# Two heads of wo loaded with 8 as the source's outermost dimension, and three short tables with 4

## The chip, the cores and the metric

The kernel runs on one core of a Trainium2 chip. The metric is the device time of one execution in microseconds (us); before the change three runs gave 1271.48, 1272.16 and 1272.31, so the median is 1272.16.

The engines are named as the profile names them: PE does matrix multiplications (PEld is its weight load), DVE is the vector engine, ACT the scalar engine, POOL is GpSimd, and SP only issues transfers and waits. Every transfer between the memory outside (HBM) and the on-chip memory (SBUF) is done by the core's 16 DMA engines. An instruction on SP or ACT describes a whole transfer; it is cut into packets that the DMA engines then carry out. In this text a "DMA engine" is one of those 16, and "engine" alone is a compute engine or SP.

## The reference

Two results are mixed by a gate. The first is one decode step of grouped-query attention: one token of width 448, 16 query heads, 8 key/value heads with 65,536 cached rows of 256 numbers each. The second is a layer norm of the token with a small two-layer map of hidden width 1792.

```python
g = sigmoid((x * gate_w).sum(-1))
q = (x @ wq).reshape(16, 256)                      # per head
p = softmax(q[h] . k_cache[h // 2] / 16)           # over 65,536 rows
a = concat_h(p @ v_cache[h // 2]) @ wo             # wo is 4096 x 448
h = layernorm(x)
b = (gelu(h[:, None] * w1[0] + b1) @ w2 + b2)      # one number for each of 448
out = g * a + (1 - g) * b
```

All inputs and the output are bf16. The two caches are 268 MB each, together 537 of the 544 MB that the kernel reads.

## The kernel before

**Blocks.** The 65,536 rows of each of the 8 key/value heads are worked off in 4 blocks of 16,384, so there are 32 blocks, n = 0 to 31 (the loop at L529). A partition holds 128 rows that follow each other in the cache, so a block's K is two tiles of 128 partitions x 64 rows (`kn0` and `kn1`, 4 MB each, loaded by `load_k`, L113), and its V is one tile of 128 x 128 rows (`vt`, 8 MB, `load_v`, L120). Each partition's share is contiguous in memory.

**A block's work.** For each of 8 groups of rows DVE transposes a piece of K (L354) and PE multiplies it with the queries (L362). After the last group comes the softmax (L416 to L455: DVE, PE and ACT by turns), and then PE multiplies the probabilities with V (L384); DVE adds the product to `acc` (L459, L464).

**Order.** Nothing is scheduled: the helper `seq` (L60) chains every instruction to the one before it on its engine, so each engine works in the order of the text. An instruction that waits holds up all that stands behind it on its engine. On SP's queue the order is: wq in two loads (L142, L143), K of block 0 in three (L152, L153), then for each block n: V of block n, the first half of K of block n+1, the second half; and at n = 0 after these the output weights wo of the first 14 heads (L541, `load_wo`, L128). V of block n is loaded when PE is done with V of block n-1, and half of K when DVE has transposed what was in its tile.

**Semaphores of loads.** Eight semaphores tell of the landing of loads, given out in turn to the loads of SP and ACT together, in the order of the text. A load that gets a semaphore again first waits until the load eight places before it has landed. In the program's list of waits this reads, for the first loads on SP: the first load of K waits for xr (L141), the second for the large part of wq (L142), the third, which is the second half of K of block 0 (L153), for w1b (L147), V of block 0 for b1b (L148), the first half of K of block 1 for w2b (L149), the second for gw (L150).

**The short tables.** ACT issues six small loads at the start: the token xr (one row of 896 bytes), w1b, b1b and w2b (L147 to L149; each 128 partitions x 14 numbers, that is 128 rows of 28 bytes), the gate's weights gw (one row of 896 bytes) and b2b (one number). DVE converts w1b and b1b at L240 and L241. Behind these two in DVE's order stand the rest of the layer norm (L242 to L250), the copies of the queries (L281, L290, L295) and all transposes of K. ACT's GELU of 14 x (128 x 448) (L255) uses both tables; PE uses w2b at L321, in `mixer_tail`, which is called in the midst of block 0.

**wo and the end of a head.** `wo_sb` holds wo with two rows (c = 0, 1) of a head on each partition: partition p of head h holds rows 2p and 2p+1 of that head's 256, 1792 contiguous bytes. When the four blocks of a key/value head are done (n = 3, 7, ...), `denominators` and `head_end` (L497) run: `collect` (L478) turns `acc` by four small matmuls, taking even columns for c = 0 and odd for c = 1, so that the product's partition p matches wo's row pair p; then `project` (L488) multiplies with wo and DVE adds up (L504, L506). The last key/value head is finished otherwise, at the program's end (L583 to L610), with wo of the last two heads loaded one by one (L550).

Of the kernel before, what the change touches and what calls it, by code (L numbers as in the profile page):

```python
# [8 lines left out]
FP32 = mybir.dt.float32  # L9
# [5 lines left out]
HQ = 16  # L15
HKV = 8
DH = 256
REP = HQ // HKV
# [6 lines left out]
NQ = 4  # L25
NW = DH // 2 // 32
QW = 128 + 2 * NI


@with_exitstack  # L30
def kernel(
# [15 lines left out]
    nc = tc.nc  # L47
# [5 lines left out]
    NF = F // 128  # L53
# [6 lines left out]
    def seq(ins):  # L60
        e = ins.ins.engine
        if e in last:
            tc.add_manual_dep(
                ins.ins,
                last[e],
                mybir.DependencyInfo(
                    mybir.DependencyClass.NoSync, mybir.DependencyReason.DATA
                ),
                reason="program order",
            )  # L70
        last[e] = ins.ins.name
        return ins
# [3 lines left out]
    work = ctx.enter_context(tc.tile_pool(name="work", bufs=1))  # L76
# [9 lines left out]
    wo_sb = const.tile([128, HQ, 2, D], BF16)  # L86
# [13 lines left out]
    w1b = const.tile([128, NF], BF16)  # L100
    b1b = const.tile([128, NF], BF16)
    w2b = const.tile([128, NF], BF16)
# [6 lines left out]
    def rows(cache, n):  # L109
        g, b = divmod(n, NB)  # L110
        return cache[0, g, b * BLK:(b + 1) * BLK, :].rearrange("(p j) d -> p j d", j=VP)
# [16 lines left out]
    def load_wo(h0, h1):  # L128
        seq(nc.sync.dma_start(
            out=wo_sb[:, h0:h1],  # L130
            in_=A_wo[h0 * DH:h1 * DH, :].rearrange("(h p c) n -> p h c n", p=128, c=2),
        ))

    def load_v_last(n):
        for j0, j1 in LAST:
            seq(nc.sync.dma_start(
                out=k_tiles[j0 // KP][:, j0 % KP:(j1 - 1) % KP + 1, :],
                in_=rows(A_v_cache, n)[:, j0:j1, :],
            ))
# [4 lines left out]
        out=wq_t[:, :], in_=A_wq[DM:D, :].rearrange("r (h n) -> (r h) n", h=2)  # L144
    ))
    with nc.allow_non_contiguous_dma(reason="short rows"):
        seq(nc.scalar.dma_start(out=w1b[:], in_=B_w1[0].rearrange("(p b) -> p b", b=NF)))  # L147
        seq(nc.scalar.dma_start(out=b1b[:], in_=B_b1.rearrange("(p b) -> p b", b=NF)))  # L148
        seq(nc.scalar.dma_start(out=w2b[:], in_=B_w2.rearrange("(p b) o -> p (b o)", b=NF)))  # L149
        seq(nc.scalar.dma_start(out=gw[:], in_=gate_w.rearrange("(o n) -> o n", o=1)))  # L150
        seq(nc.scalar.dma_start(out=b2b[:], in_=B_b2.rearrange("(o n) -> o n", o=1)))
    load_k(0, 0, ((0, 32), (32, KP)))  # L152
# [10 lines left out]
        out=val[:], in_=rowsel[:, :, :, 0:NI], op=ALU.add, axis=AXIS.XY  # L163
    ))
    fst = const.tile([128, 2, REP], FP32)
    for e in range(2):
        seq(nc.vector.tensor_reduce(
            out=fst[:, e, :], in_=rowsel[:, :, :, e:e + 1], op=ALU.add, axis=AXIS.XY
# [3 lines left out]
        out=par[:], in_=ident_f[:].rearrange("p (a r) -> p r a", r=REP), op=ALU.add, axis=AXIS.X  # L172
# [3 lines left out]
        out=nval[:], in0=val[:], scalar1=-scale, scalar2=None, op0=ALU.mult  # L176
# [7 lines left out]
        out=same[:], in_=val[:].unsqueeze(1).to_broadcast([128, 64, REP])  # L184
    ))
    seq(nc.vector.memset(pv_ps[:], 0.0))
    seq(nc.vector.memset(pv_last[:], 0.0))
    qz_tiles = [const.tile([128, 2 * NW, QW], BF16, name=f"qz{i}") for i in range(2)]
    for i in range(2):
# [3 lines left out]
        out=sel[:],  # L193
        in_=ident[:].rearrange("p (w k) -> p w k", w=NW).unsqueeze(2).to_broadcast([128, NW, NQ, 32]),
# [7 lines left out]
        out=xrr[:], in_=xr[:, DM:D].unsqueeze(2).to_broadcast([1, D - DM, 2])  # L202
    ))
    x_col = hd_ps[:, 40:44]
    for k in range(3):
# [13 lines left out]
        out=xtm[:], in0=par[:], scalar1=x_col[:, 3:4], scalar2=None, op0=ALU.mult  # L219
# [17 lines left out]
        out=veps[:], in0=mv[:, 1:2], scalar1=1e-5, scalar2=None, op0=ALU.add  # L237
# [5 lines left out]
    for _ in range(2):  # L243
# [3 lines left out]
            out=ntmp[:], in0=ntmp[:], scalar1=-0.5, scalar2=1.5, op0=ALU.mult, op1=ALU.add  # L247
# [3 lines left out]
        out=h_bc[:], in0=xf[:], scalar1=mv[:, 0:1], scalar2=rstd[:, 0:1],  # L251
        op0=ALU.subtract, op1=ALU.mult,
    ))
    for b in range(NF):
        seq(nc.scalar.activation(  # L255
            out=gel[:, b, :], in_=h_bc[:], func=ACT.Gelu_apprx_tanh,
# [4 lines left out]
    for h in range(HQ):  # L261
        half, hh = divmod(h, HQ // 2)
        for c in range(2):
            col = c * HQ + h
            for k in range(3):
                seq(nc.tensor.matmul(
                    q_ps[:, col:col + 1],
                    lhsT=wq_m[:, k, h * DH:(h + 1) * DH].rearrange("p (d c) -> p c d", c=2)[:, c, :],
                    rhs=xm[:, k:k + 1],
                    start=(k == 0),  # L270
                    stop=False,
# [3 lines left out]
                lhsT=wq_t[:, hh * DH:(hh + 1) * DH].rearrange("p (d c) -> p c d", c=2)[:, c, :],  # L275
                rhs=xtm[:, half:half + 1],
                start=False,
                stop=True,
# [4 lines left out]
    for w in range(NW):  # L283
        seq(nc.tensor.matmul(
            qq_ps[:, w * 2 * HQ:(w + 1) * 2 * HQ],
            lhsT=sel[:, w, :, :].rearrange("p a k -> p (a k)"), rhs=qb[:],
            start=True, stop=True,
# [44 lines left out]


    acc = work.tile([128, 2, DH], FP32)
    lsum = work.tile([128, 1], FP32)
    mrun = work.tile([1, REP], FP32)
    mnew = work.tile([1, REP], FP32)
# [8 lines left out]
    esc = work.tile([128, 2, REP], FP32)  # L346
# [128 lines left out]

    o_ps = [hd_ps[:, 464:464 + REP], sm_ps[:, 464:464 + REP]]

    def collect(weights, start, stop):  # L478
        for c in range(2):
            for e in range(2):  # L480
                seq(nc.tensor.matmul(  # L481
                    o_ps[c],
                    lhsT=acc[:, e, :].rearrange("p (d c) -> p c d", c=2)[:, c, :],
                    rhs=weights[:, e, :],
                    start=(start and e == 0), stop=(stop and e == 1),
                ))

    def project(g):  # L488
        a_ps = hd_ps[0:1, 0:D]
        for r in range(REP):  # L490
            for c in range(2):
                seq(nc.tensor.matmul(  # L492
                    a_ps, lhsT=oT[:, c, r:r + 1], rhs=wo_sb[:, g * REP + r, c, :],
                    start=(r == 0 and c == 0), stop=(r == REP - 1 and c == 1),
                ))

    def head_end(g):  # L497
        collect(esc, True, True)
        for c in range(2):
            seq(nc.vector.tensor_copy(out=oT[:, c, :], in_=o_ps[c]))  # L500
        project(g)
        a_ps = hd_ps[0:1, 0:D]
        if g == 0:
            seq(nc.vector.tensor_copy(out=a_acc[:], in_=a_ps))  # L504
        else:
            seq(nc.vector.tensor_tensor(out=a_acc[:], in0=a_acc[:], in1=a_ps, op=ALU.add))  # L506
# [22 lines left out]
    for n in range(NBLK):  # L529
        if n == 0:  # L530
            score_block(n, {2: gate_sum, 5: mixer_tail})
        elif n < L:
            score_block(n, {1: gate_column} if n == 1 else {})
        else:
            score_block(n, {1: result_base, 2: lambda: pv(L - 1, 0), 3: lambda: pv_one(L - 1, 2)})
        if n < L - 1:
            load_v(n)
            load_k(n + 1, 0)
            load_k(n + 1, 1)
            if n == 0:  # L540
                load_wo(0, HQ - REP)  # L541
        elif n == L - 1:
            load_v(n, 0, 48)
            load_k(L, 0)
            load_k(L, 1)
            load_v(n, 48, VP)
        else:
            load_v_last(L)
            for h in range(HQ - REP, HQ):
                load_wo(h, h + 1)  # L550
        if n < L:
            softmax(n)
        else:
            def rest_base():
                for k in range(2):
                    seq(nc.tensor.matmul(
                        f_rows[k], lhsT=ident_f[0:1, 0:1], rhs=base[0:1, k * MC:(k + 1) * MC],
                        start=True, stop=False, tile_position=(0, 32 * k),
                    ))
                pv(L - 1, 2, range(4, NJ))  # L560

            softmax(n, [lambda: pv_one(L - 1, 3), lambda: pv(L - 1, 2, range(4)), rest_base])
            seq(nc.vector.tensor_scalar(
                out=lsv[:], in0=val[:], scalar1=lsum[:, 0:1], scalar2=None, op0=ALU.mult
            ))
            pv(L - 1, 3)
            accumulate(L - 1)
            seq(nc.tensor.matmul(
                sm_ps[:, 456:456 + REP], lhsT=ones_f[:, :], rhs=lsv[:, :], start=True, stop=True
            ))  # L570
            seq(nc.vector.reciprocal(out=rdv[:], in_=sm_ps[:, 456:456 + REP]))
            seq(nc.vector.tensor_scalar(
                out=rdv[:], in0=rdv[:], scalar1=gcol[:, 0:1], scalar2=None, op0=ALU.mult
            ))
        if n < L - 1:
            if n % NB == NB - 1:
                denominators()
            products(n)
            if n % NB == NB - 1:
                head_end(n // NB)  # L580
# [6 lines left out]
    for c in range(2):  # L587
        for e in range(2):
            seq(nc.tensor.matmul(
                o_last[:, c, :],  # L590
                lhsT=acc[:, e, :].rearrange("p (d c) -> p c d", c=2)[:, c, :],
                rhs=fst[:, e, :],
                start=False, stop=False, skip_group_check=True,
# [3 lines left out]
        out=oT[:], in0=o_last, in1=rdv[:].unsqueeze(1).to_broadcast([128, 2, REP]), op=ALU.mult  # L597
    ))
    for r in range(REP):
        for c in range(2):  # L600
            for k in range(2):
# [3 lines left out]
                    start=False, stop=(r == REP - 1 and c == 1),  # L605
# [35 lines left out]
```

## Time and profile before

| what | value |
|---|---|
| median of three runs | 1272.16 us (1271.48 to 1272.31) |
| span of the profiled execution | 1270.1 us; a whole time of its own is not listed, the median is 2.06 above the span |
| PE busy | 785.6 us, 62% of the span |
| DVE busy | 683.8 us, 54% |
| ACT busy | 43.1 us, 3% |
| read from HBM | 544.22 MB, 428 GB/s over the span |
| V of a block, issue to landing | 33.3 us (median of 30) |
| half of K, issue to landing | 28.5 us (median of 63) |
| w1b, issue to landing | 10.1 us |
| b1b, issue to landing | 12.3 us |

How to read it: the profile shows one execution. A row of a compute engine gives line, operation, what it writes and reads, and how long it took; the DMA part gives the packets by queue, where q1 carries SP's loads, q10 ACT's, q8 and q14 the transfers that feed the engines with instructions and tables. The trace also holds each packet: its start, how long it took, its queue and its size, but not which of the 16 DMA engines carried it. A load ends with packets of 4 bytes, which raise its semaphore.

### The profile page before, as it was taken

Reading aid. Unit: us, or ns where it says so; the run is one execution under the profiler, and the core shown is the slowest. Engines: PE = TensorE matmul, PEld = TensorE weight load, DVE = VectorE, ACT = ScalarE, POOL = GpSimd, SP = SyncE. Lnnn points to the kernel's source line nnn. Section 1 sums busy time; section 2 is a strip of 40 time slices with the busy share of each in tenths; the row PEclk is TensorE's granted clock in tenths of the full one; section 3 lists DMA queues with packets and bytes.
Section 4 is the critical chain, followed back from the end, with each engine's and each line's share of the span. In section 5 each row is a group of like instructions: output and inputs, shape, how many; then the busy total and the mean of one; then the engine's idle time right before and its main releaser. Section 6 shows DMA issues by size and latency. Waiting matters only on the chain.

```text
span 1270.1 us, 10381 instructions
## 1 busy us (share of the span) xinstructions
PE 785.6 (62%) x4577; PEld 306.3 (24%) x4577; DVE 683.8 (54%) x619; ACT 43.1 (3%) x108; POOL 2.7 (0%) x8
## 2 busy tenths in 40 slices
PE   4656566565556666575765566655657556676566
PEld 2222222222222222122222222212222222222223
DVE  5465455665446654456554466645566444665473
ACT  4000000000000000000000000000000000000000
POOL 0000000000000000000000000000000000000000
PEclk9787778887788877878777878877887778887787
DMA  9999999999999999999999999999999999999998
GB/s 412 423 435 431 432 426 431 434 443 432 428 432 434 435 432 434 431 430 431 441 430 431 430 438 438 435 428 430 433 432 441 438 429 425 433 439 432 423 413 336
DMA packets 17989, 544.90 MB, mean 429 GB/s; under 512 B 2197, under 2 KB 4248, under 8 KB 4760
## 3 DMA queue, kind: packets, MB, share of 16 engines
q1 hardware_dynamic: 17506, 544.22, 99.4%
q8 instruction: 36, 0.59, 0.2%
q10 hardware_dynamic: 438, 0.01, 0.0%
q14 instruction: 9, 0.07, 0.0%
HBM read 544.22 MB, written 0.00 MB: 428 GB/s over the span
## 4 chain that ended last, share of the span: by engine, by line
DMA 80%; PE 15%; DVE 4%; issue 2%; ACT 0%; ACTq 0%; SPq 0%; DVEq 0%
DMA vt<-in_A_v_cache_dram 62%; DMA kn<-in_A_k_cache_dram 15%; PE pv_ps L384 11%; PE sc L362 3%; DVE kT L354 3%; DMA kn<-in_A_v_cache_dram 2%; DMA w1b<-in_B_w_dram 1%; PE hd_ps L321 0%; PE hd_ps L492 0%; PE f L602 0%; ACT p_sb L441 0%; DVE acc L459 0%; DVE pT L449 0%; DVE rmax L422 0%; DVE y_sb L325 0%
## 5 line engine op out<-in xcount | busy, mean ns | idle before, releaser
L362 PE MATMUL sc<-kT,qz 128*128 128x512 bf16 x2048 | 550.7, 419 | 246.6 <-DVE kT L354 246.4
L354 DVE STREAM_TRANSPOSE kT<-kn 128x2048 f32<-128x2048 f32 x256 | 571.2, 2282 | 128.1 <-DMA kn<-in_A_k_cache_dram 79.7
L362 PEld LDWEIGHTS <-qz 128*128 128x128 bf16 x2048 | 210.7, 104 | 586.0 <-issue 227.9
L384 PE MATMUL pv_ps<-vt,pT 128*4 128x512 bf16 x1968 | 176.0, 535 | 158.1 <-DMA vt<-in_A_v_cache_dram 156.3
L459 DVE SCALAR_TENSOR_TENSOR acc<-acc,al,pv_ps 128x512 f32<-128x512 f32 x23 | 17.2, 747 | 213.3 <-PE pv_ps L384 213.3
L384 PEld LDWEIGHTS <-pT 128*4 128x4 bf16 x2000 | 59.6, 110 | 267.1 <-issue 207.3
L441 ACT ACTIVATE p_sb<-sc,nb 128x512 bf16<-128x512 f32 x32 | 22.0, 687 | 1193.0 <-DVE nb L437 1193.0
L422 DVE TENSOR_REDUCE rmax<-sc 128x1 f32<-128x512 f32 x32 | 22.1, 691 | 60.4 <-PE sc L362 60.4
L464 DVE COPY acc<-pv_ps 128x512 f32<-128x512 f32 x8 | 5.5, 691 | 72.5 <-PE pv_ps L384 72.5
L449 DVE STREAM_TRANSPOSE pT<-p_sb 128x512 bf16<-128x512 bf16 x32 | 22.8, 711 | 28.9 <-ACT p_sb L441 28.9
L424 PE MATMUL sm_ps<-ident_f,rmax 128*1 128x128 f32 x32 | 8.7, 270 | 24.5 <-DVE rmax L422 24.5
L433 PE MATMUL sm_ps<-mrun,ones_f 1*128 1x2 f32 x64 | 12.1, 256 | 13.8 <-DVE mrun L432 11.4
L433 PEld LDWEIGHTS sm_ps<-mrun,ones_f 1*128 1x128 f32 x64 | 9.4, 182 | 20.0 <-DVE mrun L432 16.1
L437 DVE CUSTOM_DVE_ANT_0 junk<-sm_ps,nval 128x2 f32<-128x2 f32 x32 | 5.1, 159 | 15.1 <-PE sm_ps L433 15.1
L424 PEld LDWEIGHTS sm_ps<-ident_f,rmax 128*1 128x1 f32 x32 | 2.5, 79 | 40.2 <-DVE rmax L422 40.2
L467 PE MATMUL hd_ps<-lsum,same 128*128 128x1 f32 x14 | 3.5, 319 | 13.8 <-DVE lsum L451 13.8
L426 DVE TENSOR_REDUCE mnew<-sm_ps 1x2 f32<-1x64 f32 x24 | 5.1, 212 | 8.7 <-PE sm_ps L424 8.7
L255 ACT ACTIVATE wo_sb<-h_bc,b1f,w1f 128x448 bf16<-128x448 f32 x14 | 9.2, 747 | 6.7 <-DVE h_bc L250 6.7
L492 PE MATMUL hd_ps<-wo_sb,oT 128*1 128x448 bf16 x28 | 8.4, 395 | 0.0
L481 PE MATMUL hd_ps<-esc,acc 128*128 128x2 f32 x28 | 4.4, 263 | 6.0 <-DVE acc L459 6.0
L446 ACT ACTIVATE al<-nb,nb 128x1 f32<-128x1 f32 x24 | 6.8, 283 | 0.0
L506 DVE TENSOR_TENSOR a_acc<-a_acc,hd_ps 1x448 f32<-1x448 f32 x6 | 3.7, 608 | 5.5 <-PE hd_ps L492 5.5
(103 smaller groups left out, 108.2 us busy)
## 6 DMA issues: line engine op xcount, KB each, us to landing
kn<-in_A_k_cache_dram SPq DMA_DIRECT2D x63, 4096.0 KB, 28.5
vt<-in_A_v_cache_dram SPq DMA_DIRECT2D x1, 5120.0 KB, 29.9
kn<-in_A_k_cache_dram SPq DMA_DIRECT2D x2, 2048.0 KB, 12.3
kn<-in_A_v_cache_dram SPq DMA_DIRECT2D x2, 2048.0 KB, 21.2
wo_sb<-in_A_wo_dram SPq DMA_DIRECT2D x1, 3136.0 KB
vt<-in_A_wq_dram SPq DMA_DIRECT2D x1, 3072.0 KB, 10.1
vt<-in_A_v_cache_dram SPq DMA_DIRECT2D x1, 3072.0 KB
kn<-in_A_v_cache_dram SPq DMA_DIRECT2D x3, 1024.0 KB
```

What stands on the lines that cost most here:

```text
L255: seq(nc.scalar.activation(out=gel[:, b, :], in_=h_bc[:], func=ACT.Gelu_apprx_tanh, scale=w1f[:, b:b + 1], bias=b1f[:, b:b + 1],))
L354: seq(nc.vector.transpose(out=kT_tiles[i % 2][:].rearrange("p j w k c -> p (j w k c)").bitcast(FP32), in_=k_tiles[i // 4][:, i % 4 * NJ:(i ...
L362: seq(nc.tensor.matmul(sc_tiles[n % 2][:, :], lhsT=qz_tiles[n // NB % 2][:, 2 * w + c, 2 * (NI - i):2 * (NI - i) + 128], rhs=kT_tiles[i % ...
L384: seq(nc.tensor.matmul(dst[32 * grp:32 * grp + 2 * REP, :, :], lhsT=pT[:, 32 * jj + 2 * REP * ip:32 * jj + 2 * REP * (ip + 1)], rhs=pairs( ...
L422: seq(nc.vector.tensor_reduce(out=rmax[:], in_=sc_ps[:, :], op=ALU.max, axis=AXIS.X))
L424: seq(nc.tensor.transpose(sm_ps[0:1, 0:128], rmax[:, 0:1], ident_f[:, :]))
L433: seq(nc.tensor.matmul(sm_ps[:, 128:128 + REP], lhsT=ones_f[0:1, :], rhs=mrun[0:1, :], start=True, stop=True))
L441: seq(nc.scalar.activation(out=p_sb[:, :], in_=sc_ps[:, :], func=ACT.Exp, scale=scale, bias=nb[:, 0:1], accum_out=den[:, 0:1],))
L446: seq(nc.scalar.activation(out=al[:], in_=nb_old[:], func=ACT.Exp, scale=-1.0, bias=nb[:, 0:1]))
L449: seq(nc.vector.transpose(out=pT[:, :], in_=p_sb[:, :]))
L459: seq(nc.vector.scalar_tensor_tensor(out=acc[:], in0=acc[:], scalar=al_tiles[n % 2][:, 0:1], in1=src[:, :, :], op0=ALU.mult, op1=ALU.add,))
L492: seq(nc.tensor.matmul(a_ps, lhsT=oT[:, c, r:r + 1], rhs=wo_sb[:, g * REP + r, c, :], start=(r == 0 and c == 0), stop=(r == REP - 1 and c ...
```

## The change

The loads of w1b, b1b and w2b name their 128 rows of 28 bytes in another order: the source is walked as 4 x 32 rows with the 4 outermost, row 4q + a in place of row p = 32a + q. wo of the first two heads (h = 0, 1, the pair of the first key/value head) is loaded head by head with a source walked as 8 x 16 row pairs, 8 outermost: partition 16a + b holds row pair 8b + a. The other twelve heads are loaded as before in one transfer. On SP one load at L541 becomes three. In the three tables the new order is the same for all of them, so that the sum over the hidden width is over the same numbers. For wo, the end of the first key/value head has to deliver its product in the new order: two copies on ACT write `acc` into `acc_sp` with the columns rearranged, and `collect` reads that. The instruction order on each engine is otherwise the same; the two copies stand on ACT between the softmax of block 3 and that of block 4.

```diff
+WA = 8
+GA = 1
+FA = 4
...
+    def load_wo_outer(h):
+        seq(nc.sync.dma_start(
+            out=wo_sb[:, h].rearrange("p c n -> p (c n)"),
+            in_=A_wo[h * DH:(h + 1) * DH, :].rearrange("(b a c) n -> a b (c n)", a=WA, c=2),
+        ))
...
-        seq(nc.scalar.dma_start(out=w1b[:], in_=B_w1[0].rearrange("(p b) -> p b", b=NF)))
-        seq(nc.scalar.dma_start(out=b1b[:], in_=B_b1.rearrange("(p b) -> p b", b=NF)))
-        seq(nc.scalar.dma_start(out=w2b[:], in_=B_w2.rearrange("(p b) o -> p (b o)", b=NF)))
+        seq(nc.scalar.dma_start(out=w1b[:], in_=B_w1[0].rearrange("(q a b) -> a q b", a=FA, b=NF)))
+        seq(nc.scalar.dma_start(out=b1b[:], in_=B_b1.rearrange("(q a b) -> a q b", a=FA, b=NF)))
+        seq(nc.scalar.dma_start(out=w2b[:], in_=B_w2.rearrange("(q a b) o -> a q (b o)", a=FA, b=NF)))
...
+    acc_sp = work.tile([128, 2, 2, 128], FP32)
...
-                    lhsT=acc[:, e, :].rearrange("p (d c) -> p c d", c=2)[:, c, :],
+                    lhsT=acc_sp[:, e, c, :] if spread else
+                    acc[:, e, :].rearrange("p (d c) -> p c d", c=2)[:, c, :],
...
     def head_end(g):
-        collect(esc, True, True)
+        if g < GA:
+            for e in range(2):
+                seq(nc.scalar.copy(
+                    out=acc_sp[:, e].rearrange("p c (a b) -> p c a b", a=WA),
+                    in_=acc[:, e, :].rearrange("p (b a c) -> p c a b", a=WA, c=2),
+                ))
+        collect(esc, True, True, g < GA)
...
             if n == 0:
-                load_wo(0, HQ - REP)
+                for h in range(GA * REP):
+                    load_wo_outer(h)
+                load_wo(GA * REP, HQ - REP)
```

More of the change, by code (lines that the diff above doesn't have):

```diff
@@ L476, with collect @@
     o_ps = [hd_ps[:, 464:464 + REP], sm_ps[:, 464:464 + REP]]
-    def collect(weights, start, stop):
+    def collect(weights, start, stop, spread=False):
         for c in range(2):
```

## The prediction

> **What bounds the kernel now.** I read the page's DMA part and the chain that ended last, then the timeline of the start, then SP's waits, then the end.
>
> ```profile
> DMA  9999999999999999999999999999999999999998
> ...
> q1 hardware_dynamic: 17506, 544.22, 99.4%
> q8 instruction: 36, 0.59, 0.2%
> q10 hardware_dynamic: 438, 0.01, 0.0%
> ...
> DMA 80%; PE 15%; DVE 4%; issue 2%; ACT 0%; ACTq 0%; SPq 0%; DVEq 0%
> ```
>
> The 16 DMA engines are full from end to end and 80% of the chain is loads. In steady state a packet of 32768 bytes follows the last on its DMA engine after 1.21 us: 27.1 GB/s, times 16 is 433. So compute counts only where it makes a load's issue so late that a queue runs dry. V of block 2 is issued at 104.29 and lands 33.1 later; its own 8 MB need 19.4, so 13.7 us of work lay ahead of it. That is the cover of a usual block.
>
> The chain's end depends on the slowest DMA engine. The trace doesn't number them, but each engine's packets can be followed, since each starts where its last one ended. The start times of the 16 completion packets (4 bytes) of two loads of V:
>
> ```
> V of block 0:  49.77 49.84 49.93 49.94 49.98 50.02 50.04 50.05 50.10 50.20 50.26 50.32 50.48 50.61 50.86 51.75
> V of block 29: 1179.57 1179.70 1179.98 1180.14 1180.22 1180.23 1180.28 1184.73 1185.24 1185.37 1185.40 ... 1185.68
> ```
>
> Seven stay together, nine fall behind by 5 to 6 us. Eight of the nine carry the instruction fetches on q8 in turn: at 241.79 one lost 0.95 us to a fetch and its next packet took 0.47 more than the usual 2.42, so 1.41 per fetch, four times each by 1180. The ninth carries the table transfers of q14, 0.84 each. At the end the rate falls while the nine finish alone; these are the DMA and rate lines of 1262 to 1270, in slices of 0.2 us:
>
> ```profile
> DMA  9988846555565544121211100000000040000000
> GB/s 506 397 316 320 297 184 236 211 201 227 215 234 215 198 188 152 68 82 72 81 63 63 45 0 0 0 0 0 0 0 0 0 82 4 0 0 0 0 0 0
> ```
>
> The seven end near 1262.5 to 1263.0, the fetching ones at 1265.0 to 1266.6, and the output waits for these.
>
> **The start**, timeline and SP's waits up to 60 us:
>
> ```profile
> 1.29 0.37 ACTq L147 DMA_DIRECT2D w1b<-in_B_w_dram  x1
> 2.09 9.61 SPq L115 DMA_DIRECT2D kn<-in_A_k_cache_dram  x3
> ...
> 11.38 0.17 DVE L240 CAST w1f<-w1b 128x14 f32<-128x14 bf16 x1 [3.23 <-DMA w1b<-in_B_w_dram]
> ...
> 14.01 0.17 DVE L241 CAST b1f<-b1b 128x14 f32<-128x14 bf16 x1 [2.45 <-DMA b1b<-in_B_b_dram]
> ```
> ```profile
> SPq L121 <- DMA b1b<-in_B_b_dram: 2.3, 1, 2.3
> ...
> SPq L115 <- DMA w1b<-in_B_w_dram: 0.2, 1, 0.2
> ```
>
> SP's third K load (half `kn1`) starts at 11.38, the moment w1b lands: it takes over w1b's semaphore. V of block 0 likewise follows b1b. Both land late because a DMA engine takes q1 and q10 by turns, one packet each; one engine's rows (start, end):
>
> ```
> 5.265 5.274 q10 28 B
> 5.271 6.183 q1 24576 B
> 6.180 6.189 q10 28 B
> 6.185 7.097 q1 24576 B
> ```
>
> A table is 128 rows and 16 completions, 9 packets on each DMA engine, so it needs about 8 large packets of q1 to pass.
>
> **Change 1, the tables.** Loads of 128 rows end with 16 completion packets, the one-row loads (xr, gw, output) with one: the outermost count sets how many DMA engines share a load. I take it that 4 gives 4 engines, 8 gives 8. [...]
>
> Each of four DMA engines then has 32 + 1 packets per table. The first q10 packet comes after q1's third or fourth (5.27 to 5.99), and the 33rd after 32 more: 5 of wq and its completion, 8 + 1 of wq's tail, 8 + 1 and 8 of the first half of K. That is the end of all that is on SP's queue, 20.8 to 21.6 in the trace (the completions of that K load, one straggler with a fetch at 22.75). The slowest of four is at about 21.45; from last completion to issue took 0.37 at w1b (11.00 to 11.38). So the third K load is issued at 21.8 and not 11.38, when all 16 queues are empty. What a restart costs is shown once: at 1206.22 SP issued K while seven DMA engines ran dry; their first packets started at 1207.2 to 1207.3 and took 0.7 to 1.1 longer than usual, so the flow stood 1.9 after the issue. Flow again at 23.7. The fetching engines, free at 20.76 to 21.27, lose 2.65 on average; the straggler 0.95. Bounds: nothing (w1b not later) to 10 (rival B).
>
> What waits behind: b1b's and w2b's packets have the gap for themselves, 66 packets per DMA engine; a 28-byte packet held the next up by 6 ns, a 1792-byte one by 70, so they take 0.4 to 4.6 us, and I take under 1 (28 bytes is the nearer row). b1b lands near 22.1 where it was 14.0, and DVE, with the layer norm, the queries and every transpose of K behind L241, runs 8.1 late, PE's scores and ACT's GELU with it. K of block 1 is issued at 37.6 and not 29.5; V of block 0 flows until 23.7 + 9.7 + 19.4 = 52.8 and covers that. Its second half goes from 50.8 to about 55.6 (tile 1 is worked off in 17.9 from the end of tile 0), under K's first half until 62.5. V of block 1 goes from 62.5 to about 67.3, under K and wo until 79. So nothing more runs dry.
>
> **Change 2, wo.** A row pair of wo costs 70 ns (113 packets in 7.92). Two heads are 16 per DMA engine, 1.1 us. Afterwards eight DMA engines carry 32 and eight none: -1.1 for these, +1.1 for the others. Which eight? The one-row load gw (packet of 896 bytes at 18.361) sits on an engine that I can follow, with one near-tie at 53.54, into the seven; if loads on few engines start at the same end, the seven include that end. I take -1.1 for the fetching engines; bounds -1.1 and +1.1. The extra two issues on SP (0.39 each at L129) come 5 us before SP's next wait ends, and cost nothing.
>
> **Change 3, the copies.** Two ACT copies of 128x256 stand between L459 and L481 at n = 3: at 0.69 for 128x512 (L441), 0.35 to 0.69 each; about 1 us later for PE, DVE and V of block 4's issue, once. The cover is 13.7 us; without it, 1 us.
>
> **Sum.** The last to end now: the straggler (1266.63), which gets 0.95 - 1.1 = -0.15, and two others with a fifth fetch late (1266.3 to 1266.56), which get 2.65 - 1.1 = +1.55 and end at about 1268.0. The q14 engine (1264.56), if among the lower eight, gets 2.65 + 1.1, loses 0.9 of it in a dry spell at 1219, and ends at 1267.4. So 1268.0 against 1266.63: +1.35. On the span of 1270.1 that gives 1271.45; the median stands 2.06 above it, so **1273.5**. A measurement of this kernel can tell about 0.2%, 2.54 us; this is no change within it.
>
> **Rivals.**
> A, wo falls on the fetching engines (they are not the upper half): +1.1 in place of -1.1 for at least some. 1273.5 + 2.2 = 1275.7, slower. For: the trace shows only that one engine doesn't fetch. Chance 0.15.
> B, the small packets don't get through in the gap, slower: the gap is 1.7 us to the first new packet, so above 52 ns per packet b1b's 33 are not done; the rest go one by one between K packets of 1.21. b1b lands near 34, V of block 0 is issued with all queues empty (about 3 lost), DVE starts 20 late, and the second half of K of block 1 comes about 4 after the queue is dry. 1273.5 + 7 = 1280.5. Against: 6 ns. Chance 0.12.
> C, the tables are not late: a turn of q10 takes many packets, w1b lands before 11, nothing runs dry. Then only change 2 is left: 1272.2 - 1.1 = 1271.1; if loads stay on 16 engines after all, 1272.2. [...] Chance 0.18.
>
> **How the numbers follow.** Forecast 0.55, of which 0.10 lies above 1274.7 (a restart or a fourth engine later than taken); A 0.15, B 0.12, C 0.18, of which 0.05 for a gain of over 2.5 that I can't name but in the lag of 5 to 6 us. Slower by over 0.2%: 0.10 + 0.15 + 0.12 = 0.37; faster 0.05; within 0.45 + 0.13 = 0.58. The range takes in C's 1271.1 and A's 1275.7 with 1.3 for the restart's spread at the top, and leaves out B: 1270.8 to 1277.0.
>
> **What would show it.** w1b's landing at 20 or later and SP's third K load with it; a hole in the DMA line at 21 to 23.5; L241 near 22; 33 packets per table on four DMA engines; K and V of block 1 issued without a hole. At the end the spread between the seven and the nine shrinks by 2.2; if it grows, A. w1b before 12 is C, a second hole at 33 is B. Wrong altogether if DVE or PE sets the issue of loads in a later block.

## The result, and the profile after

The changed kernel takes **1275.74 us** (median of 7 runs, 1275.40 to 1278.21), the kernel before 1272.07 beside it (7 runs, 1271.48 to 1272.39): a ratio of 1.0033, 95% interval 1.0022 to 1.0043. The profiled execution took 1275.72, its span is 1273.7. The forecast was 1273.5, no change within 0.2%. The kernel came out 2.2 us slower than that, inside the range of 1270.8 to 1277.0; but the slowing is clear of 0.2%, and to that the prediction had given a chance of 0.37. Which of its steps failed is the matter of what follows.

The page of the changed kernel, its line of DMA shares, its queues and the chain that ended last:

```profile
DMA  9999999999999999999999999999999999999998
...
q1 hardware_dynamic: 17522, 544.22, 99.3%
q8 instruction: 35, 0.57, 0.2%
q10 hardware_dynamic: 402, 0.01, 0.0%
...
DMA 79%; PE 15%; DVE 3%; issue 1%; ACT 0%; SPq 0%; DVEq 0%
```

The bound is the same: DMA engines full from end to end. q10, the tables' queue, has 36 packets fewer. Three tables with 16 completion packets each had 48 of these; with 4 each they have 12, and that is the 36. So 4 outermost does mean 4 DMA engines. q1 has 16 more: one load with 16 completions has become three with 8, 8 and 16. So 8 outermost means 8.

**The start.** The timeline of all engines up to 23 us (start, duration, engine, line):

```profile
1.29 0.62 ACTq L156 DMA_DIRECT2D w1b<-in_B_w_dram  x1
...
2.02 20.22 SPq L118 DMA_DIRECT2D kn<-in_A_k_cache_dram  x3
...
3.37 13.98 ACTq L159 DMA_DIRECT2D gw<-in_gate_w_dram  x1
...
21.91 0.17 DVE L249 CAST w1f<-w1b 128x14 f32<-128x14 bf16 x1 [13.76 <-DMA w1b<-in_B_w_dram]
22.08 0.17 DVE L250 CAST b1f<-b1b 128x14 f32<-128x14 bf16 x1
...
22.36 0.35 SPq L124 DMA_DIRECT2D vt<-in_A_v_cache_dram  x1
```

w1b lands at 21.9 and no longer at 11.4. SP's third K load goes out with it (the row at 2.02 holds three issues and ends at 22.24), and b1b is there by 22.08. SP's list of waits names the reason:

```profile
SPq L118 <- DMA w1b<-in_B_w_dram: 10.6, 1, 10.6
```

SP's timeline after that, with the loads of block 1 and of wo:

```profile
37.44 15.65 SPq L118 DMA_DIRECT2D kn<-in_A_k_cache_dram  x2
53.18 1.43 SPq L138 DMA_DIRECT2D wo_sb<-in_A_wo_dram  x2
54.66 0.45 SPq L132 DMA_DIRECT2D wo_sb<-in_A_wo_dram  x1
64.43 11.58 SPq L124 DMA_DIRECT2D vt<-in_A_v_cache_dram  x1
```

**Two holes in the rate.** Two stretches of the changed kernel (the columns end with the granted clock, the DMA share and GB/s; a packet counts whole where it starts, so a share can pass 1):

```profile
20.00:24.00 4.00, 0.00 (x0) 0.00 (x0) 1.77 (x12) 1.40 (x2) 0.00 (x0) 1.00 0.72 227
72.00:77.00 5.00, 2.44 (x11) 1.06 (x11) 5.00 (x3) 0.00 (x0) 0.00 (x0) 1.00 1.00 222
```

and the same two of the kernel before:

```profile
20.00:24.00 4.00, 3.78 (x9) 1.26 (x9) 2.53 (x3) 4.00 (x7) 0.00 (x0) 1.00 1.09 471
72.00:77.00 5.00, 3.38 (x15) 1.44 (x15) 5.00 (x3) 0.00 (x0) 0.00 (x0) 1.00 1.05 407
```

The first is the hole that was forecast: the DMA share falls to 0.72. The second was not forecast, and it is of another kind. The share stays at 1.00, so the DMA engines are busy, but they move 222 GB/s in place of 407. The packets tell why. Before, each row pair of wo (1792 bytes) took 74 ns, from 69 to 79 us. After, from 72.2 to 77.7, 574 of them took more than 85 ns, 133 on average, on all 16 DMA engines (15 to 18 of these packets ran at a time, for 4.0 us in all), also on the eight that were carrying the load of the other twelve heads in its unchanged form. Summed over all packets and divided by 16, that is 2.16 us of each DMA engine above 74 ns a packet.

**The end.** The changed kernel from 1266 to 1274 us, in slices of 0.2, four us later than the stretch shown of before:

```profile
DMA  8988665555333323321110000000000000000000
GB/s 333 385 341 294 229 243 191 220 230 223 123 122 115 133 113 129 134 108 54 54 54 9 0 0 0 0 0 0 0 0 0 0 4 0 0 0 0 0 0 0
```

The last load's last completion comes at 1270.30 where it came at 1266.63: 3.67 later, which is the whole difference of the medians (also 3.67). The tail is longer at the low end (the 54 at 1269.6 to 1270.2 is two DMA engines alone), because the DMA engines have drifted further apart. The sixteen completions of a K load that begin at 1125:

```
after : 1125.4 1125.8 | 1127.7 1127.7 1128.0 1128.2 1128.3 | 1129.7 1129.8 1129.8 1131.1 1131.3 1131.5 | 1132.6 1133.4 1133.4
```

The spread is 8.0 us, as it is in the V load that follows; before, it was 6.1. Two DMA engines without fetches and without the extra row pairs of wo lead; five carry the extra row pairs; six carry fetches; the last three carry both (one of these the transfers of q14, which the page lists as instruction, like q8's). That reading of who carries what is from following packets, and is likely, not certain.

### The profile page after: what moved, and what is told of

It reads as the page before. It is cut to its first block, busy times and chain, and to the rows that moved or that the text cites. A ratio compares the mean times of both kernels' runs of the same rounds, so it can differ in the third digit from the quotient of the medians.

```text
span 1273.7 us, 10384 instructions
## 1 busy us (share of the span) xinstructions
PE 778.1 (61%) x4577; PEld 305.0 (24%) x4577; DVE 684.0 (54%) x619; ACT 44.2 (3%) x110; POOL 2.7 (0%) x8
## 4 chain that ended last, share of the span: by engine, by line
DMA 79%; PE 15%; DVE 3%; issue 1%; ACT 0%; SPq 0%; DVEq 0%
DMA vt<-in_A_v_cache_dram 73%; PE pv_ps L394 12%; DMA kn<-in_A_k_cache_dram 4%; DVE kT L364 2%; PE sc L372 2%; DMA kn<-in_A_v_cache_dram 2%; PE hd_ps L330 0%; PE f L621 0%; PE hd_ps L503 0%; ACT p_sb L451 0%; DVE acc L469 0%; DVE pT L459 0%; DVE rmax L432 0%; DVE y_sb L334 0%; PE hd_ps L491 0%
## 5 line engine op out<-in xcount | busy, mean ns | idle before, releaser
L394 PE MATMUL pv_ps<-vt,pT 128*4 128x512 bf16 x1968 | 170.4, 521 | 161.6 <-DMA vt<-in_A_v_cache_dram 159.8
L432 DVE TENSOR_REDUCE rmax<-sc 128x1 f32<-128x512 f32 x32 | 22.1, 692 | 60.8 <-PE sc L372 60.8
L443 PE MATMUL sm_ps<-mrun,ones_f 1*128 1x2 f32 x64 | 12.1, 257 | 13.8 <-DVE mrun L442 11.4
L477 PEld LDWEIGHTS hd_ps<-lsum,same 128*128 128x128 f32 x14 | 3.5, 311 | 14.4 <-DVE lsum L461 14.4
```

What stands on the lines that cost most here:

```text
L394: seq(nc.tensor.matmul(dst[32 * grp:32 * grp + 2 * REP, :, :], lhsT=pT[:, 32 * jj + 2 * REP * ip:32 * jj + 2 * REP * (ip + 1)], rhs=pairs( ...
L432: seq(nc.vector.tensor_reduce(out=rmax[:], in_=sc_ps[:, :], op=ALU.max, axis=AXIS.X))
L443: seq(nc.tensor.matmul(sm_ps[:, 128:128 + REP], lhsT=ones_f[0:1, :], rhs=mrun[0:1, :], start=True, stop=True))
L477: seq(nc.tensor.matmul(hd_ps[:, 460:461], lhsT=same[:].rearrange("p a r -> p (a r)"), rhs=lsum[:, 0:1], start=True, stop=True,))
```

## The experiments

Every kernel was timed against the kernel before on the same chip. "Packets" are always the 1792-byte ones of wo around 70 to 82 us, and slow packets are those of more than 85 ns. Each diff is cut to the lines that matter.

**Which part costs what.** First, the tables alone (wo as before) and wo alone (tables as before).

```diff
-GA = 1
+GA = 0
```

> The three tables walked with 4 outermost, wo as in the kernel before. Theory (two costs: the tables hold the second half of K of block 0 until 21.9, about 2.6 us; wo's two heads make every DMA engine's 1792-byte packets take 140 ns for 4 us): here only the first, K issued at 21.9, wo's packets 74 ns, time 1272.1 + 2.5 = 1274.6 (1274.0 to 1275.2). Rival A as it was put (the tables cost what was forecast and the rest is wo's place on fetching engines): the same 1274.6. Rival (the tables cost nothing, since the DMA engines that lose the 2.6 us have idle time later): 1272.1.

Measured: 1274.15 (11 runs) against 1271.67, ratio 1.0019 [1.0011, 1.0028], +2.5 us. Packets 74 ns. SP's timeline of this kernel is that of the changed kernel:

```profile
2.08 19.95 SPq L118 DMA_DIRECT2D kn<-in_A_k_cache_dram  x3
22.16 0.35 SPq L124 DMA_DIRECT2D vt<-in_A_v_cache_dram  x1
37.52 15.66 SPq L118 DMA_DIRECT2D kn<-in_A_k_cache_dram  x2
```

So the tables cost about what the forecast gave for the hole.

```diff
-in_=B_w1[0].rearrange("(q a b) -> a q b", a=FA, b=NF)
+in_=B_w1[0].rearrange("(p b) -> p b", b=NF)
```

(b1b and w2b alike.)

> wo of two heads with 8 outermost and the two copies on ACT, tables as before. Theory: 1792-byte packets take about 140 ns on all 16 DMA engines while the two heads load (4.5 us), so the eight that carry no part of them win 1.1 and lose 2.3, the others lose 1.1 + 2.4: 1272.1 + 1.2 to 1.6, 1273.3 to 1273.7. Rival A (packets normal, the place alone): the fetching engines among the lower eight lose 1.1: up to 1273.2, and then packets at 74 ns. If my first reading of the place were right and packets were normal: 1271.0.

Measured: 1274.04 (11 runs), ratio 1.0015 [1.0007, 1.0024], +2.4 us by the medians, where the forecast's step would have given a gain. The slow packets took 112 on average, not 140. The rate from 70 to 74 us, of this kernel and in the second line of the kernel before:

```profile
70.00:74.00 4.00, 1.53 (x8) 0.77 (x7) 3.22 (x3) 0.00 (x0) 0.00 (x0) 1.00 1.01 267
70.00:74.00 4.00, 1.53 (x9) 0.75 (x8) 3.10 (x3) 0.00 (x0) 0.00 (x0) 1.00 1.01 392
```

It moves 267 GB/s, where the kernel before moves 392. The slow packets come with wo alone. Added up, +2.5 and +2.4 are more than the +3.67 of both together, but the two intervals (1.4 to 3.6 and 0.9 to 3.1) allow it. The median spans, which leave out the time around the program, give less to wo: 1272.0 with the tables alone and 1270.8 with wo alone, against 1269.6, so +2.4 and +1.2; with both the span is 1273.7.

**Why the packets are slow: how wo is read.** Three kernels change what is read, in place of the interleaved row pairs of 8 DMA engines.

```diff
-in_=A_wo[h * DH:(h + 1) * DH, :].rearrange("(b a c) n -> a b (c n)", a=WA, c=2)
+in_=A_wo[0:2 * DH, :].rearrange("(a s c) n -> a s (c n)", a=WA, c=2)[:, 16 * h:16 * (h + 1), :]
```

> Tables as before; the two heads are loaded with 8 outermost, but each of the 8 DMA engines reads 16 row pairs that follow each other in memory, and the eight start 57 KB apart. The first key/value head's product is then taken with rows of wo in the wrong places, which changes no time. Theory R (the doubling comes from the reads: eight engines side by side within 14 KB of the source): packets at 74 ns, only the place is left, 1272.1 to 1273.2. Theory W (it comes from the writes: eight engines that each write 16 neighbouring partitions): 140 ns again, the time of wo alone.

Measured: 1273.44 (10 runs), ratio 1.0015 [1.0006, 1.0024]; packets of 74 to 186 ns, mean of the slow packets 110, from 70.0 to 76.0. Reading neighbouring row pairs doesn't help, and Theory R falls.

```diff
-WA = 8
+WA = 16
```

> Tables as before; the two heads are loaded with 16 outermost in the same interleaved order (partition 8a + b holds row pair 16b + a), so all 16 DMA engines share them again, and the place is as before. Theory R: the reads are side by side again (16 engines within 28 KB), packets 140 ns for 16 packets on every engine, 1272.1 + 1.1 = 1273.2. Theory W: each engine writes 8 partitions as in any load, 74 ns, 1272.1, and the two copies on ACT and the two extra loads cost nothing either.

Measured: 1273.35 (10 runs), ratio 1.0010 [1.0001, 1.0020]; slow packets of 108 on average from 70.05 to 74.2.

```profile
70.00:74.00 4.00, 2.90 (x13) 1.27 (x12) 1.06 (x2) 0.00 (x0) 0.00 (x0) 0.93 1.00 266
```

So it isn't that only eight DMA engines share the load. Theory W falls as it was put, with 74 ns for 16 outermost; it had taken it that each DMA engine then writes the same partitions as in any load, and the last experiment comes back to that.

With 8 outermost again, but the DMA engines 458 KB apart:

```diff
+in_=A_wo.rearrange("(a b c) n -> a b (c n)", a=WA, c=2)[:, h * 16:(h + 1) * 16, :]
```

> The tables as before; the two loads with 8 outermost, but each of the 8 DMA engines reads 16 neighbouring row pairs from another part of wo, 458 KB from the next engine's (the product of the first key-value head takes wrong rows of wo). Theory H (reads crowded into one head): the packets take 74 ns again, since no two DMA engines read within 458 KB of each other, and the time is 1271.5 to 1272.8. Theory F (the form of the load with an extra outer dimension): packets of 110 to 140 ns as with the rows interleaved, and the time is 1273.3 to 1274.2, as when wo alone was changed (1274.04).

Measured: 1273.65 (10 runs), ratio 1.0010 [1.0001, 1.0020]; slow packets of 105 on average from 70.0 to 76.0. Theory H falls: none of the distances tried between the reads, from 1.8 KB to 458 KB, makes them quick.

**Or the load of a single head, or the form.** The next two keep the loads plain (two dimensions).

```diff
-load_wo(0, HQ - REP)
+load_wo(0, 1)
+load_wo(1, 2)
+load_wo(2, HQ - REP)
```

> The tables as before; wo's first two heads each in a load of their own, but in the plain order of before (all 16 DMA engines, one row pair per partition), without any copy. Theory H (what halves the rate is that all DMA engines read within one head's 229 KB at a time, while the load of fourteen heads steps 229 KB from packet to packet): the 1792-byte packets of the two heads take 100 to 140 ns as in the runs with 8 and 16 outermost, the two heads take about 1 us longer on all 16 DMA engines, and the time is 1272.9 to 1273.7. Theory F (it is the load with the extra outer dimension itself): the packets take 74 ns as in before, and the time is that of before, 1271.5 to 1272.3 (two more loads on SP's queue cost nothing that the queue's stock of several loads would not cover).

Measured: 1271.78 (10 runs) against 1271.87, ratio 0.9999 [0.9989, 1.0008]; packets 74 ns, and from 70 to 74 us

```profile
70.00:74.00 4.00, 2.08 (x11) 0.96 (x9) 1.89 (x2) 0.00 (x0) 0.00 (x0) 1.00 1.03 398
```

And in place of the load with 16 outermost, one of two dimensions with the same step between row pairs:

```diff
+in_=A_wo.rearrange("(p x c) n -> p x (c n)", p=128, c=2)[:, h, :]
```

> The tables as before; the two heads each in a load of two dimensions, as the plain loads of one head, but partition p reads row pair 16 p + h: each step 28,672 bytes, the step of the load with 16 outermost, over the whole of wo (the product of the first key-value head takes wrong rows). Theory F (the form): 74 ns. Theory P (the distance in wo): over 90 ns on all DMA engines for the some 2 us of these packets.

Measured: 1271.58 (one run); packets 74 ns, 391 GB/s:

```profile
70.00:74.00 4.00, 1.80 (x9) 0.87 (x8) 2.17 (x2) 0.00 (x0) 0.00 (x0) 1.00 1.01 391
```

A load of two dimensions is quick at both steps in wo that were tried. The counterpart, almost the plain rows in the form with an extra dimension (16 outermost, 9 row pairs apart):

```diff
+in_=A_wo[h * DH:h * DH + 288, :].rearrange("(a b c) n -> a b (c n)", a=WA, c=2)[:, 0:8, :]
```

> As wo with 16 outermost (tables as before), but each of the 16 DMA engines reads 8 neighbouring row pairs, and the engines lie 9 row pairs apart instead of 8: almost the rows of the plain load of one head, in the form with an extra outer dimension (the product of the first key-value head takes some wrong rows). Theory F (the form of the load): 1792-byte packets of 95 to 130 ns on all DMA engines as with 16 outermost interleaved, time 1272.8 to 1273.7. Theory P (the distance in wo between what the DMA engines read at one time, which was plain in none of the slow runs): 74 ns, as with the plain loads of one head, time 1271.5 to 1272.4.

Measured: 1273.22 (10 runs), ratio 1.0011 [1.0002, 1.0021]; slow packets of 107 on average from 70.0 to 74.2:

```profile
70.00:74.00 4.00, 2.34 (x11) 1.06 (x10) 1.62 (x2) 0.00 (x0) 0.00 (x0) 1.00 1.03 276
74.00:78.00 4.00, 2.90 (x13) 1.25 (x13) 4.00 (x3) 0.00 (x0) 0.00 (x0) 1.00 1.05 402
```

Theory P falls: of the orders of reading that were tried, none makes the difference, and Theory F (the form) stood after this. A larger dose, all fourteen heads, in that form and plainly:

```diff
-load_wo(0, HQ - REP)
+for h in range(HQ - REP):
+    load_wo_outer(h)
```

> All fourteen heads of wo in loads of their own with 16 outermost and 9 row pairs between the DMA engines, tables as before (seven times the packets of the run with two such heads; the products of the first seven key-value heads take some wrong rows). Theory F (every packet of a load with the extra outer dimension slows all 16 DMA engines while it lasts): 1792-byte packets of 100 to 130 ns from first to last, some 70 to 82 us, where before ended at 78; 112 packets for each DMA engine at 30 to 50 ns more are 3.4 to 5.6 us, the time 1275 to 1277.5. Rival (only the first such packets cost, while the DMA engines are out of step with the K packets ahead): slow until 74 and then 74 ns, 1272.8 to 1273.7 as with two heads.

Measured: 1276.12 (5 runs) against 1271.87, ratio 1.0033 [1.0020, 1.0046], +4.25 us. Slow from 69.9 to 82.6: packets of some 125 until 72.5, then of some 95 to the end, 3.05 us in sum for each DMA engine, somewhat under the 3.4 to 5.6 expected. So it is not only the first packets that are slow. The packets of 65,536 bytes that followed took up to 3938 ns beside them, where 2418 is usual.

> The same fourteen loads of one head each in the plain two-dimensional form, tables as before. Theory F: 74 ns throughout and the time of before, 1271.3 to 1272.4. Rival (it is the number of loads, each with its own issue and completion): packets between the loads held up, as late as the run with the extra dimension, 1273 to 1277.

Measured: 1272.27 (10 runs), ratio 1.0004 [0.9994, 1.0013]. The number of loads is not the cause. But not all is 74 ns here: 42 packets between 73.4 and 78.0 took 285 on average, 0.55 us in sum, while SP was still giving out the last seven of these loads (71.9 to 75.6; it had waited for semaphores). These few long packets are not the even slowness of the other runs, and what they are was not tried. Packets of 65,536 bytes took up to 3622 ns here too, so long ones of that size are no mark of the rearranged form by themselves.

**Or what is written.** One thing had gone along with the form in all runs: to which partitions a DMA engine writes. With 8 or 16 outermost and 128 partitions it writes 16 or 8 neighbouring ones in a row, if each DMA engine takes one step of the outermost dimension; no trace shows which partitions a packet goes to. The last kernel keeps the form with 8 outermost and changes that.

```diff
+in_=A_wo[h * DH + 2 * p0:h * DH + 2 * p1, :].rearrange("(b a c) n -> a b (c n)", a=8, c=2)
...
+for h, p0, p1 in ((0, 0, 32), (0, 32, 64), (1, 0, 32), (1, 32, 64), (0, 64, 128), (1, 64, 128)):
+    load_wo_part(h, p0, p1)
+load_wo(REP, HQ - REP)
```

> The tables as before, no copies; the two heads of wo in six loads with 8 outermost: first partitions 0 to 31 and 32 to 63 of each head (four loads; a DMA engine writes 4 neighbouring partitions of each, 16 packets in all), then partitions 64 to 127 of each head (two loads; 8 neighbouring partitions each, 16 packets in all). Inside a load the row pairs stand in another order, so the product of the first key-value head takes wrong rows. Theory S (what slows is which partitions are written at one time: in the slow loads each DMA engine writes 8 or 16 neighbouring partitions, and so several write into partitions that the plain loads keep apart): the first 16 packets of a DMA engine take 74 ns, and so do those of the other eight meanwhile; the second 16 are slow, 100 to 145 ns. The slow stretch is half as long as when all of wo's two heads stood so (2 us in place of 4 to 6), and the time 1272.4 to 1273.4. Theory F (the form with an extra outer dimension is slow whatever is written): slow from the first such packet to the last, 4 to 6 us, and the time 1273.3 to 1274.5. [...]

Measured: 1273.42 (10 runs) against 1271.99, ratio 1.0009 [0.9999, 1.0019]. The mean of packets in each half microsecond:

```
us      69.0 69.5 70.0 70.5 71.0 71.5 72.0 72.5 73.0 73.5 74.0 74.5 75.0 75.5 76.0
ns        74   74   74   74  107  134  138  122  118  110  104   98   96   77   74
```

From the first packet at 69.3 to 71.0 all are at 74. In the other runs with 8 or 16 outermost and the tables as before, the first slow packet came 0.6 to 0.8 us after the first packet of wo; here it came 1.7 us after it, at 71.03. The DMA engines that began at 69.3 had by 70.5 (16 packets of 74 ns) gone through the four loads to partitions 0 to 63, and then came to the loads of 64 to 127, with 8 neighbouring partitions for each. The first slow packet came about half a microsecond after that. With these loads the mean of all packets rises to 138 ns (72.0 to 72.5). Three stretches of this kernel:

```profile
69.50:71.50 2.00, 1.15 (x6) 0.58 (x5) 0.81 (x2) 0.00 (x0) 0.00 (x0) 1.00 0.99 347
72.00:76.00 4.00, 2.59 (x12) 1.09 (x12) 4.00 (x3) 0.00 (x0) 0.00 (x0) 1.00 1.05 286
76.00:78.00 2.00, 1.71 (x9) 0.70 (x8) 2.00 (x2) 0.00 (x0) 0.00 (x0) 1.00 1.36 545
```

The first four loads have the extra outer dimension too and ran quick, so Theory F falls as it was put ("slow from the first such packet"), and the order of events is that of Theory S, which puts it on the arrangement of the partitions written at one time. The two groups of loads differ in three things, though: four or eight neighbouring partitions for each DMA engine, partitions 0 to 63 or 64 to 127, and loads of 32 or of 64 partitions; they also stood in one order only. Which of these it is was not tried. Theory S's size was not right either. The slow stretch was 4.7 us and not 2, and by the time alone, which lies at the edge of both forecasts, the two are not told apart; the onset in one profiled execution is what speaks for S. Why the partitions written should matter shows in no trace. Two more things the runs do not give: why the other eight DMA engines are slowed as much (133 on average for all in the changed kernel), and why packets stay slow with one DMA engine left at the rearranged loads (in the changed kernel from 76.64 to 77.21, and the packets of 76.7 to 77.2 took 93 on average). In the runs with 8 or 16 outermost the slowness ends 0.5 to 0.7 us after the last completion of these loads (73.59 and 74.20 with 16, 75.48 and 76.04 with 8 and 458 KB apart, 77.21 and 77.74 in the changed kernel), though by then most DMA engines had gone on (in the changed kernel 15 of these loads' 16 completions had come by 76.64).

**Why the tables could get through at all.** The changed kernel with gw and b2b issued ahead of the three tables:

```diff
+seq(nc.scalar.dma_start(out=gw[:], in_=gate_w.rearrange("(o n) -> o n", o=1)))
+seq(nc.scalar.dma_start(out=b2b[:], in_=B_b2.rearrange("(o n) -> o n", o=1)))
 seq(nc.scalar.dma_start(out=w1b[:], in_=B_w1[0].rearrange("(q a b) -> a q b", a=FA, b=NF)))
```

> The changed kernel with one thing moved: ACT issues gw and b2b ahead of the three tables, so that SP's third K load follows w2b's or another load's semaphore and not w1b's. Theory G (the wait of SP for w1b is what keeps the queue small enough for the tables to get through; its price is the hole of 2.6 us): the third K load goes out near 11 us, no hole, and the tables of b1b and w2b, packet by packet beside 32 KB packets on their four DMA engines, land near 40 to 60 us; L249 and L250 on DVE, and the passes of block 0 behind them, come that late, K of block 1 is issued 10 to 20 us later than in the changed kernel's 37.4, and the time is 1280 to 1295. Rival (the tables are quick whoever waits, as the 66 packets before 21.4 us at 5.9 ns each suggest): b1b lands before 25 us, no hole, and the time is 1272.5 to 1274, about that of the two heads of wo alone.

Measured: 1298.9 (one run), +27. Rows from its timeline of 20 to 70 us:

```profile
25.16 0.17 DVE L249 CAST w1f<-w1b 128x14 f32<-128x14 bf16 x1 [17.01 <-DMA w1b<-in_B_w_dram]
51.25 0.18 DVE L250 CAST b1f<-b1b 128x14 f32<-128x14 bf16 x1 [25.92 <-DMA b1b<-in_B_b_dram]
...
66.78 0.33 SPq L118 DMA_DIRECT2D kn<-in_A_k_cache_dram  x1
```

and from 52 to 64 us the DMA engines move nothing:

```profile
52.00:64.00 12.00, 6.80 (x22) 2.68 (x22) 9.82 (x18) 10.37 (x15) 0.00 (x0) 1.00 0.00 0
```

Theory G holds, but its sizes were too low: the time lies above its 1280 to 1295, and K of block 1 is later than its 10 to 20 us. SP's third K load no longer waits for w1b (it is out by 11.8), so no hole arises at 21; b1b's packets go one by one beside K's and V's packets of 32 and 64 KB, land at 51, and K of block 1 is issued 29 us later than in the changed kernel, long after the queue is empty.

## Why the prediction was near, and what failed in it

**The tables: right.** Third K load 21.91 (forecast 21.8), L250 22.08 (22.1), K of block 1 37.44 (37.6). Its second half went out somewhat sooner than forecast, at 52.8 (55.6), and V of block 1 at 64.43 (67.3). The completions of the third K load come at 33.2 to 33.7 where they came at 30.5 to 31.3, with one straggler at 32.4: +2.6 for most (2.65), and the tables alone cost +2.5 by the medians. In their profiled execution it is less, +1.65 at the last completion (1268.28 against 1266.63): I take it that which DMA engine is last depends on the fetches it got (one fetch cost 1.41 in the kernel before). Nothing else ran dry before wo, as forecast (DMA share 0.99 from 24 to 60 us, 1.01 from 60 to 72). The turns of one packet each carried this, and rival C falls: its turns of many packets show in no run, and w1b landed at 21.9. As long as q1 had packets, the tables' alternated with them one by one, on four DMA engines as on 16: on one of the four they start at 6.226, 7.140, 8.054 and 8.968, with a q1 packet of 912 ns between each two. Only with q1 empty, from 21.0 on the first of the four and by 21.4 on all, did they go back to back.

**B: off.** From 21.4 on the 28-byte packets follow each other after 5.9 ns; b1b is there within 0.2 us of w1b. That the packets were the danger is shown by the run with gw ahead, where the gap is missing.

**The copies: right.** They take 1.14 us of ACT, under the cover:

```profile
187.89 1.14 ACT L511 COPY acc_sp<-acc 128x256 f32<-128x256 f32 x2 [9.87 <-DVE acc L469]
```

**wo: this is the step that failed**, "A row pair of wo costs 70 ns", and with it "-1.1 for these, +1.1 for the others" and "I take -1.1 for the fetching engines". The 70 ns came from rows of a load in its plain form, and the rearranged load was priced with it. Its packets cost 133 on average, and the others' in that time too: 2.16 us for each DMA engine, and 1.35 + 2.16 = 3.51 is near the +3.67 that came. So the forecast's second term has the wrong sign: wo alone is +2.4 by the medians, +1.2 by the spans, and not a gain.

**A: true in part, and not the reason.** Its 1275.7 is the time that came, and some fetching engines do seem to carry extra row pairs, but the slow packets, which it knew nothing of, are the larger part: the match of the number is luck. That loads on few DMA engines take a "lower eight", or start at the same end, shows in no run, since the trace doesn't number the DMA engines; what following the packets gave, as likely, is that of the eight with extra row pairs five carry no fetches, two do and one carries q14's transfers. Take the last completion's shift in the profiled executions with wo alone changed and subtract the packets' time over 74 ns:

| kernel | last completion later by | packets over 74 ns, per DMA engine | rest |
|---|---|---|---|
| 8 outermost | 0.63 | 1.31 | -0.7 |
| 8, neighbouring rows | 2.65 | 1.94 | +0.7 |
| 8, 458 KB apart | 2.62 | 1.72 | +0.9 |
| 16 outermost | 1.25 | 1.26 | 0.0 |
| 16, 9 row pairs apart | 1.29 | 1.24 | +0.1 |

With 16 outermost, where every DMA engine carries its usual share if 16 gives 16 as 4 gave 4 and 8 gave 8, the slow packets make up the whole cost. With 8, a rest of -0.7 to +0.9 remains, inside the bounds of -1.1 and +1.1 that were given for the place. Each row is one execution, and the spans of the kernel before alone range from 1269.1 to 1270.4. By the median spans the place shows no cost: 8 outermost is 1.2 to 1.5 above the kernel before, 16 outermost 1.4 to 1.7. But the executions with 8 outermost scatter more, with spans of 1270.2 to 1272.9 against 1270.8 to 1271.6. Which DMA engine gets a late fetch seems to decide; that was not shown. As for "the spread shrinks by 2.2", it grew from 6.1 to 8.0; by the reading above, since the engines that end last carry both fetches or q14's transfers and the extra rows.

What stays open: which property of these loads makes the packets slow (the partitions written, as the onset in one execution suggests, or another), why a load on eight DMA engines slows the packets of all 16, and what the 42 long packets with fourteen plain loads are.

## What to carry to other kernels

A rearranged load must not be priced by the packet time of the plain one (here 133 ns on average for the slow packets, and not 74): try it alone, with what each DMA engine writes in view, since a load that kept the DMA engines busy here still nearly halved the rate of all (222 GB/s in place of 407). A DMA share of 1.00 with little over half the GB/s was the sign of that here, a share below 1 (0.72) that of a dry queue. And a short table on few DMA engines, behind large packets, landed here when the large ones were through (w1b at 21.9 in place of 11.4; with gw ahead, b1b at 51, and from 52 the DMA engines move nothing): look up which load waits for its semaphore, since that wait may be the price or, as here, the lesser one.

## What the runs showed that I had not expected

ACT was held up for 13.98 us in issuing gw (the row at 3.37). At that time the three tables' 99 packets for each of four DMA engines stood on its queue; before, with some 27 for each of 16, the same issue took 0.43:

```profile
2.87 0.43 ACTq L150 DMA_DIRECT2D gw<-in_gate_w_dram  x1
```

That the number of packets is the reason was not tried. It cost nothing here, since DVE waited until 21.9 for w1b anyway, but ACT's own work (L248) came at 19.9 in place of 8.2.

Small packets of the rearranged form beside large ones did no harm by themselves: with gw ahead, K's packets of 32 KB took 1213 and V's of 64 KB 2418 ns, as ever, while b1b's ran beside them for 25 us, two to three packets a microsecond in all four.
